# Linear attention beside a gated product: one ones column per four heads in kv, q projected one tile sooner, tile 0's epsilon on VectorE

## The chip, the cores and the metric

The kernel runs on one core of a Trainium2 chip. The time is device microseconds for one execution of the whole program. Before the change three runs gave 221.94, 222.10 and 222.32 us, with a median of 222.1 us.

## What is computed

The input x has 2048 tokens of 512 numbers in bf16. It is normalised per token, and the result feeds two branches whose outputs are added to x.

```
xn = (x - mean) / sqrt(var + 1e-5)
# branch A: linear attention, 32 heads of 16
q, k, v = split(xn @ wqkv)
phi(t)  = concat(softmax(t @ w_phi), softmax(-t @ w_phi))   # 32 features per head
kv  = sum over tokens of phi(k)^T v        # per head 32 x 16
z   = sum over tokens of phi(k)            # per head 32
o   = (phi(q) @ kv) / (phi(q) @ z + 1e-6)
A   = o @ wo
# branch B: gated product, hidden width 1792
B   = ((xn @ w_gate) * (xn @ w_up)) @ w_down
out = x + A + B
```

## The kernel before

The 2048 tokens are 16 tiles of 128 tokens (`NT = 16`). All instructions are issued in an order written out by hand: within each engine they run in the order in which the Python code names them, and an engine whose next instruction waits does nothing else meanwhile. The output of matrix products goes to PSUM: a pool `ps_s` gives six banks in rotation to every projection (`bank(...)`), and two more banks belong first to the kv accumulators (`ps_k`) and later to the numerators (`ps_ab`).

**Start.** Tiles 0 to 3 are normalised one by one: VectorE takes sums (L155, `stats`) and the mean and variance (L347, `mv`); GpSimd adds epsilon (L164, `ve`) and raises to the power -0.5 (L166, `rstd`); VectorE applies both (L171, `xn`). TensorE transposes the tile (L213, `tp`), and ScalarE copies it out (L215, `xnT`). Ten matmuls on zeros (`warm`, L307) keep TensorE running while x arrives.

**Stage k and v.** For each tile `vproj` projects v and evicts it into a buffer `vt` (L322; five buffers, with ones columns set once, L138). `kproj` computes the features of k. `kv(n)` then adds phi(k)^T v over the tokens into PSUM: eight matmuls (L333), one per group of four heads. Group `gr` has the 4 x 32 = 128 features of its heads as rows. Its 68 columns are, for each of the four heads, 16 columns of v and a column of ones, which gives z. Between these steps stand "units" of branch B (`ffn(k)`): a unit is eight matmuls (`g` and `u`, L275), a copy of g on ScalarE (L279, `g_sb`) and a product on VectorE (L280, `hT`).

**Turn to the numerators.** After the last kv, two VectorE products (L419) multiply the accumulators by a mask M4 that keeps each row's own head, and write `KV` to SBUF with 17 columns per head. Then come `qproj(4)`, one unit, and the numerators' stage. There `attend(n)` computes eight matmuls of 68 columns (L430) into `ab`, of which there is one buffer (two banks). VectorE then adds 1e-6 to the denominators (L435, `den`), takes reciprocals (L437, `rden`) and writes the quotient (L439, `otok`). A DMA transposes that into `oT` (L442).

**q.** `qproj(n)` takes the features of q: four matmuls (L240), two exponentials on ScalarE (L248 and L249, `e`), sums and reciprocals on VectorE (L252 `sums`, L254 `rs`), the product on GpSimd (L256, `phiq`), and a transposing DMA on SyncE's queue (L263) into one of six `phiqT` buffers. q of tiles 0 to 3 is made among the last k and v tiles.

**Numerators' stage.** The loop at its end is:

```
for n in range(NT):
    attend(n)
    if n + 5 < NT:
        qproj(n + 5)
    if n < 2:
        ffn(2 - n)
        continue
    fin(n - 2)
    if n >= 4:
        ffn(2)
```

`fin(n)` adds the products of `hT` with w_down and of `oT` with wo (L293, L296, 18 matmuls of 512 columns), adds x on VectorE (L299, `o_sb`) and stores the tile (L300).

Of the kernel before, what the change touches and what calls it, by code (L numbers as in the profile page):

```python
# [8 lines left out]
BF16 = mybir.dt.bfloat16  # L9
F32 = mybir.dt.float32  # L10
AF = mybir.ActivationFunctionType
ALU = mybir.AluOpType
# [4 lines left out]
def _bcast_ap(ap_in: bass.AP, new_ap):  # L17
    return bass.AP(tensor=ap_in.tensor, offset=ap_in.offset, ap=new_ap)
# [3 lines left out]
def kernel(  # L22
# [12 lines left out]
    nc = tc.nc  # L35
    P = 128
# [3 lines left out]
    DH = D // H  # L40
    NT = S // P
    DC = D // P
    FC = F // P
    EPS = 1e-5
    GT = 4
    NGRP = NT // GT
    TT = GT * P
    E1 = DH + 1

    def token_views(ap):  # L50
        rows = ap.flatten_outer_dims()
        first = rows[0:TT, :].rearrange("(n p) d -> p n d", p=P)
        rest = rows[TT:S, :].rearrange("(p n) d -> p n d", p=P)
        return lambda lo, hi: first[:, lo:hi, :] if hi <= GT else rest[:, lo - GT:hi - GT, :]
# [4 lines left out]
    consts = ctx.enter_context(tc.tile_pool(name="consts", bufs=1))  # L59
# [27 lines left out]
    for lo in (0, 2):  # L87
        nc.sync.dma_start(out=wv[:, lo:lo + 2, :],
                          in_=A_wqkv[lo * P:(lo + 2) * P, 2 * D:3 * D].rearrange("(c p) f -> p c f", p=P))
# [27 lines left out]

    BO = consts.tile([P, 8, E1], BF16)
    nc.gpsimd.memset(BO[:], 1.0)
    _block_rows(nc.gpsimd, BO[:], 8, DH, E1)  # L120
    NG = H // 4
    KV = wpool.tile([P, NG, 4, E1], BF16)
    M4 = consts.tile([P, 4, E1], BF16)

# [9 lines left out]
    NV = 5  # L134
    vts = []
    for i in range(NV):
        vt = consts.tile([P, 8, 4, E1], BF16, name=f"vt{i}")
        nc.vector.memset(vt[:, :, :, DH:E1], 1.0)  # L138
        vts.append(vt)

    gpool = ctx.enter_context(tc.tile_pool(name="gpool", bufs=3))
# [17 lines left out]
        stats = ln_sums(n)  # L159
        nc.vector.bn_aggr(out=mv, in_=stats[:])  # L160

    def ln_rstd(mv, k):
        ve = lnpool.tile([P, GT], F32, name="ve")
        nc.gpsimd.tensor_scalar(out=ve[:, 0:k], in0=mv[:, 0:k, 1], scalar1=EPS, scalar2=None, op0=ALU.add)  # L164
        rstd = lnpool.tile([P, GT], F32, name="rstd", bufs=GT)
        nc.gpsimd.tensor_tensor(out=rstd[:, 0:k], in0=ve[:, 0:k], in1=mhalf[:, 0:k], op=ALU.pow)  # L166
        return rstd
# [92 lines left out]
    def qproj(n):  # L260
        phiq = features(n, W1q, "q")
        phiqTs[n] = qtpool.tile([P, NG, P], BF16, name="phiqT")
        nc.sync.dma_start(out=phiqTs[n][:], in_=phiq[:].rearrange("p g c -> p (g c)"), transpose=True)  # L263
# [18 lines left out]
    def ffn(k):  # L282
        for _ in range(k):
            if units:
                unit(*units.pop(0))
# [23 lines left out]
    warm_up(10)  # L309

    with tc.tile_pool(name="ps_k", bufs=1, space=PSUM) as ps_k:
        kvps = [ps_k.tile([P, 4, 4, E1], F32, name=f"kv{b}") for b in range(2)]
        phiks = {}

        def vproj(n, copy=nc.scalar.copy, amid=None, later=False):
            ps = bank("pv")
            proj(ps, n, wv, range(2))
            if amid is not None:
                amid()
            proj(ps, n, wv, range(2, DC))  # L320
            def evict():
                copy(out=vts[n % NV][:, :, :, 0:DH], in_=ps.rearrange("p (a b c) -> p a b c", a=8, b=4))  # L322
            if later:
                return evict
            evict()

        def kproj(n):
            phiks[n] = features(n, W1k, "k")

        def kv(n):  # L330
            vt, phik = vts[n % NV], phiks[n]
            for gr in range(NG):
                nc.tensor.matmul(kvps[gr // 4][:, gr % 4, :, :].rearrange("p a b -> p (a b)"),  # L333
                                 lhsT=phik[:, gr, :], rhs=vt[:, gr, :, :].rearrange("p a b -> p (a b)"),
                                 start=(n == 0 and gr % 4 == 0), stop=(n == NT - 1 and gr % 4 == 3))

        mvs = [mv_tile() for n in range(GT)]
        rstds = []

        def first_apply(n):  # L340
            ln_apply(n, mvs[n][:, 0, 0:1], rstds[n][:, 0:1])

        def first_stats(n, amid=None):
            stats = ln_sums(n)
            if amid is not None:
                first_apply(amid)
            nc.vector.bn_aggr(out=mvs[n][:, 0, :], in_=stats[:])  # L347
            rstds.append(ln_rstd(mvs[n], 1))

        first_stats(0)  # L350
        first_stats(1)
        first_apply(0)
        first_stats(2, amid=1)
        first_stats(3, amid=2)
        first_apply(3)
        make_bd()
        nc.gpsimd.tensor_tensor(out=M4[:], in0=BO[:, 0:4, :], in1=BO[:, 4:8, :], op=ALU.add)
        lt(0, parts=2)
        warm_up(1)
        vproj(0, amid=lambda: lt(1, parts=2))  # L360
        copy_v = vproj(1, later=True)
        lt(2)
        copy_v()
        unit(0, 0, 0, 2 * P)
        vproj(2, copy=nc.vector.tensor_copy, amid=lambda: lt(3))
        unit(0, 1, 0, 2 * P)
        vproj(3, copy=nc.vector.tensor_copy)
        for f in range(2):
            unit(0, f, 2 * P, TT)
        del units[0:2]  # L370
        ffn(1)
        for j0 in (0, 2):
            fold(1, W1k, j0, (nc.scalar.copy, nc.vector.tensor_copy))
        ffn(1)
        ln_block(4)
        ffn(1)
        chore(2)
        kproj(0)
        ffn(1)
        chore(2)  # L380
        ffn(1)
        chore()
        kproj(1)
        ffn(1)
        chore()
        ffn(1)
        kproj(2)
        chore()
        ffn(1)
        kv(0)  # L390
        chore()
        ffn(1)
        kproj(3)
        chore()
        ffn(1)
        kv(1)
        nc.sync.dma_start(out=wT2[:, 0, :, :], in_=A_wqkv[:, 0:D], transpose=True)
        for n in range(GT, NT):
            if n in (4, 8):
                ln_block(n + 4)  # L400
            vproj(n)
            kproj(n)
            chore(1 if n % GT < 2 else 0)
            ffn(1)
            kv(n - 2)
            chore((1, 2, 2, 2)[n % GT])
            if n >= 8 and n % 2 == 0:
                qproj((n - 8) // 2)
            if n == 6:
                fold(0, W1q, 0)  # L410
            ffn(1)
            if n == 6:
                fold(0, W1q, 2)
        ffn(1)
        kv(NT - 2)
        ffn(1)
        kv(NT - 1)
        for b in range(2):
            nc.vector.tensor_tensor(out=KV[:, 4 * b:4 * b + 4, :, :], in0=kvps[b][:],  # L419
                                    in1=_bcast_ap(M4[:], [M4[:].ap[0], [0, 4], [E1, 4], [1, E1]]), op=ALU.mult)  # L420
        qproj(4)
        ffn(1)

    with tc.tile_pool(name="ps_ab", bufs=1, space=PSUM) as ps_ab, \
            tc.tile_pool(name="dp", bufs=2) as dpool:

        def attend(n):
            ab = ps_ab.tile([P, 2, TT], F32, name="ab")
            for gr in range(NG):
                nc.tensor.matmul(ab[:, gr // 4, (gr % 4) * 4 * E1:(gr % 4 + 1) * 4 * E1],  # L430
                                 lhsT=phiqTs[n][:, gr, :], rhs=KV[:, gr, :, :].rearrange("p a b -> p (a b)"),
                                 start=True, stop=True)
            abv = ab[:, :, 0:16 * E1].rearrange("p b (h j) -> p b h j", j=E1)
            den = dpool.tile([P, 2, 16], F32, name="den")
            nc.vector.tensor_scalar(out=den[:], in0=abv[:, :, :, DH], scalar1=1e-6, scalar2=None, op0=ALU.add)  # L435
            rden = dpool.tile([P, 2, 16, 1], F32, name="rden")
            nc.vector.reciprocal(out=rden[:, :, :, 0], in_=den[:])  # L437
            o_tok = dpool.tile([P, D], BF16, name="otok")
            nc.vector.tensor_tensor(out=o_tok[:].rearrange("p (b h d) -> p b h d", b=2, d=DH),  # L439
                                    in0=abv[:, :, :, 0:DH], in1=rden[:].to_broadcast((P, 2, 16, DH)), op=ALU.mult)  # L440
            oTs[n] = otpool.tile([P, DC, P], BF16, name="oT")
            nc.sync.dma_start(out=oTs[n][:], in_=o_tok[:], transpose=True)  # L442

        for n in range(NT):
            attend(n)
            if n + 5 < NT:
                qproj(n + 5)
            if n < 2:
                ffn(2 - n)
                continue  # L450
# [3 lines that stand above are left out]
        ffn(len(units))  # L454
        fin(NT - 2)
        fin(NT - 1, cuts=(0, 3 * P, D))
# [30 lines left out]
```

## Time and profile before

| | value |
|---|---|
| median of three runs | 222.1 us |
| the profiled execution's own time | 221.94 us |
| its span, first to last instruction | 220.2 us |
| TensorE busy | 214.5 us (97%) |
| VectorE busy | 138.4 us (63%) |
| ScalarE busy | 88.2 us (40%) |
| GpSimd busy | 72.1 us (33%) |
| mean granted TensorE clock | 0.998 |

The stages lie in the span as follows; the columns are busy us of each engine in that stretch, from the trace by windows.

| stretch, us | what runs | TensorE | VectorE | ScalarE | GpSimd |
|---|---|---|---|---|---|
| 0 to 8.3 | start | 6.62 | 4.84 | 3.31 | 4.36 |
| 8.3 to 109.2 | v, k, kv, units, q 0 to 3 | 100.27 | 70.44 | 61.68 | 44.51 |
| 109.2 to 111.7 | KV, q 4, one unit | 2.45 | 1.41 | 1.14 | 0.00 |
| 111.7 to 119.6 | attend 0 and 1, q 5 and 6, three units | 7.85 | 7.56 | 4.14 | 3.87 |
| 119.6 to 138.5 | attend from 2 on, fin | 18.80 | 12.78 | 4.43 | 7.74 |
| 138.5 to 188.9 | attend, q, fin, two units per tile | 50.14 | 30.00 | 13.54 | 11.61 |
| 188.9 to 217.5 | attend, fin | 28.41 | 11.10 | 0.00 | 0.00 |

A timeline line gives the start in us, the duration in us, the engine (PE is TensorE, PEld its weight loads, DVE is VectorE, ACT is ScalarE, POOL is GpSimd, SP is SyncE), the line of the code and the tiles. What stands in brackets is the engine's idle time before it and what ended it. A matmul's duration includes its way through the array; the start of the next one tells how long it holds the engine.

### The profile page before, as it was taken

What the parts mean: (1) busy time and instruction counts of PE and PEld (TensorE: products, weight loads), DVE (VectorE), ACT (ScalarE), POOL (GpSimd) and SP (SyncE); (2) the same over time, 40 slices, a digit from 0 to 9 for tenths busy, and PEclk for the clock granted to TensorE, in tenths of its full rate; (3) what the DMA queues carried; (4) which work ended last, traced back from release to release, by engine and by line L of the source; (5) the groups of instructions that cost most, each with busy time, mean ns of one, the idle gap of its engine ahead of it and who ended that gap; (6) DMA issues with size and microseconds to landing.
All of it is one profiled execution on the core that took longest, in us unless ns stands there. A gap on an engine that the chain in (4) does not pass through costs nothing.

```text
span 220.2 us, 3489 instructions
## 1 busy us (share of the span) xinstructions
PE 214.5 (97%) x1285; PEld 104.4 (47%) x1309; DVE 138.4 (63%) x237; ACT 88.2 (40%) x162; POOL 72.1 (33%) x62
## 2 busy tenths in 40 slices
PE   7999999999999999999999999999999999999995
PEld 2564444445444444444544444444444444454443
DVE  5657985885579685756589964197655745445321
ACT  2635486559755876545354221231322323100000
POOL 5300555455336653536333633033033033000000
PEclk9999999999999999999999999999999999999999
DMA  5999994404201223010205945214431431522611
GB/s 171 261 306 383 368 225 59 95 1 49 49 0 33 42 54 65 18 34 0 48 1 100 119 95 113 58 24 95 98 72 24 95 71 27 91 53 71 69 30 48
DMA packets 47233, 19.91 MB, mean 90 GB/s; under 512 B 37488, under 2 KB 46960, under 8 KB 47088
## 3 DMA queue, kind: packets, MB, share of 16 engines
q1 hardware_dynamic: 47216, 19.69, 39.6%
q8 instruction: 10, 0.16, 0.3%
q14 instruction: 7, 0.06, 0.1%
HBM read 8.67 MB, written 2.10 MB: 49 GB/s over the span
## 4 chain that ended last, share of the span: by engine, by line
PE 94%; DVE 2%; DMA 1%; issue 1%; POOL 0%; ACT 0%; DVEq 0%
PE fin L293 22%; PE u L275 22%; PE g L275 21%; PE fin L296 6%; PE pv L240 6%; PE q L240 6%; PE k L240 6%; PE ab L430 2%; PE kv L333 2%; DMA xall<-in_A_x_dram 1%; DVE stats L155 1%; PE pq L231 1%; DVE sums L252 1%; PE tp L213 0%; DVE hT L280 0%
## 5 line engine op out<-in xcount | busy, mean ns | idle before, releaser
L275 PE MATMUL u<-xnT,wu 128*128 128x512 bf16 (+1 forms) x229 | 57.7, 372 | 0.4
L275 PE MATMUL g<-xnT,wg 128*128 128x512 bf16 (+1 forms) x222 | 56.7, 371 | 0.4
L280 DVE TENSOR_TENSOR hT<-u,g_sb 128x512 bf16<-128x512 f32 (+1 forms) x58 | 37.4, 649 | 27.3 <-PE u L275 18.0
L279 ACT CAST g_sb<-g 128x512 bf16<-128x512 f32 (+1 forms) x58 | 33.3, 573 | 48.2 <-PE g L275 48.1
L252 DVE TENSOR_REDUCE sums<-e 128x64 f32<-128x1024 f32 x32 | 38.9, 1215 | 20.7 <-ACT e L249 20.7
L293 PE MATMUL fin<-wd,hT 128*128 128x512 bf16 (+2 forms) x234 | 50.9, 366 | 0.3
L256 POOL TENSOR_TENSOR phiq<-e,rs 128x1024 bf16<-128x1024 f32 x16 | 31.0, 1935 | 61.4 <-DVE rs L254 53.1
L256 POOL TENSOR_TENSOR phik<-e,rs 128x1024 bf16<-128x1024 f32 x16 | 30.9, 1934 | 48.2 <-DVE rs L254 46.2
L275 PEld LDWEIGHTS <-wu 128*128 128x128 bf16 x232 | 22.6, 98 | 25.7
L293 PEld LDWEIGHTS <-hT 128*128 128x128 bf16 x238 | 22.4, 98 | 24.8
L275 PEld LDWEIGHTS <-wg 128*128 128x128 bf16 x232 | 21.9, 98 | 23.4
L240 PEld LDWEIGHTS <-xnT 128*128 128x128 bf16 x192 | 17.3, 97 | 18.2 <-ACT xnT L215 1.1
L299 DVE TENSOR_TENSOR o_sb<-fin,xall 128x512 bf16<-128x512 f32 (+2 forms) x17 | 11.2, 656 | 22.3 <-PE fin L296 22.2
L248 ACT ACTIVATE e<-q 128x512 f32<-128x512 f32 x16 | 9.5, 596 | 26.1 <-PE q L240 20.7
L254 DVE RECIPROCAL rs<-sums 128x64 f32<-128x64 f32 x32 | 17.7, 553 | 3.1
L240 PE MATMUL pv<-wv,xnT 128*128 128x512 bf16 x62 | 16.4, 379 | 0.4 <-ACT xnT L215 0.2
L296 PE MATMUL fin<-wo,oT 128*128 128x512 bf16 (+2 forms) x68 | 16.6, 366 | 0.0
L240 PE MATMUL k<-W1k,xnT 128*128 128x512 bf16 x63 | 16.2, 379 | 0.0
L240 PE MATMUL q<-W1q,xnT 128*128 128x512 bf16 x60 | 15.9, 378 | 0.1
L322 ACT CAST vt<-pv 128x512 bf16<-128x512 f32 x14 | 8.3, 591 | 10.9 <-PE pv L240 10.9
L248 ACT ACTIVATE e<-k 128x512 f32<-128x512 f32 x16 | 9.6, 597 | 7.0 <-PE k L240 6.6
L439 DVE TENSOR_TENSOR otok<-ab,rden 128x512 bf16<-128x512 f32 x16 | 11.1, 691 | 0.6
(46 smaller groups left out, 117.4 us busy)
## 6 DMA issues: line engine op xcount, KB each, us to landing
out_dram<-o_sb SPq DMA_DIRECT2D x15, 128.0 KB, 1.9
wd<-in_B_w_down_dram SPq DMA_DIRECT2D x1, 1792.0 KB, 15.4
wg<-in_B_w_gate_dram SPq DMA_DIRECT2D x2, 640.0 KB, 7.0
wu<-in_B_w_up_dram SPq DMA_DIRECT2D x2, 640.0 KB, 8.1
xall<-in_A_x_dram SPq DMA_DIRECT2D x1, 1024.0 KB, 12.0
wv<-in_A_wqkv_dram SPq DMA_DIRECT2D x2, 256.0 KB, 3.9
wg<-in_B_w_gate_dram SPq DMA_DIRECT2D x2, 256.0 KB, 4.9
wu<-in_B_w_up_dram SPq DMA_DIRECT2D x2, 256.0 KB, 5.3
```

The costliest lines, as they stand in the source:

```text
L240: nc.tensor.matmul(ps, lhsT=xnT[:, j, n * P:(n + 1) * P], rhs=w[:, j, :], start=(j == 0), stop=(j == DC - 1))
L248: nc.scalar.activation(out=e[:, :, 0, :], in_=pfv, func=AF.Exp, scale=1.0)
L252: nc.vector.tensor_reduce(out=sums[:], in_=ev, axis=AX.X, op=ALU.add)
L254: nc.vector.reciprocal(out=rs[:].rearrange("p a b -> p (a b)"), in_=sums[:])
L256: nc.gpsimd.tensor_tensor(out=phi[:].rearrange("p g (x f) -> p (g x) f", f=DH), in0=ev, in1=rs[:].to_broadcast((P, 2 * H, DH)), op=ALU.mult)
L275: nc.tensor.matmul(ps, lhsT=w[:, c, f * P:(f + 1) * P], rhs=xnT[:, c, T * TT + lo:T * TT + hi], start=(c == 0), stop=(c == DC - 1))
L279: nc.scalar.copy(out=g_sb[:, 0:hi - lo], in_=pss[0])
L280: nc.vector.tensor_tensor(out=hTs[T][:, f, lo:hi], in0=pss[1], in1=g_sb[:, 0:hi - lo], op=ALU.mult)
L293: nc.tensor.matmul(ps, lhsT=hTs[T][:, f, t4 * P:(t4 + 1) * P], rhs=wd[:, f, lo:lo + w], start=(f == 0), stop=False)
L296: nc.tensor.matmul(ps, lhsT=oTs[n][:, c, :], rhs=wo[:, c, lo:lo + w], start=False, stop=(c == DC - 1))
L299: nc.vector.tensor_tensor(out=o_sb[:], in0=ps, in1=xall[:, n, lo:lo + w], op=ALU.add)
L439: nc.vector.tensor_tensor(out=o_tok[:].rearrange("p (b h d) -> p b h d", b=2, d=DH), in0=abv[:, :, :, 0:DH], in1=rden[:].to_broadcast((P, ...
```

## The change

Three edits. `vt` gets 65 columns per group of four heads, 64 of v and one of ones, so that a kv matmul has 65 columns in place of 68. The mask step then makes the 16 columns per head and the z column in two VectorE instructions for each accumulator, four in place of two. `qproj(5)` is called ahead of `attend(0)`, and after each `attend(n)` stands `qproj(n + 6)` in place of `qproj(n + 5)`. The epsilon of tile 0 is added by VectorE; that of all other tiles stays on GpSimd.

```diff
+    G1 = 4 * DH + 1
...
-        vt = consts.tile([P, 8, 4, E1], BF16, name=f"vt{i}")
-        nc.vector.memset(vt[:, :, :, DH:E1], 1.0)
+        vt = consts.tile([P, NG, G1], BF16, name=f"vt{i}")
+        nc.vector.memset(vt[:, :, 4 * DH:G1], 1.0)
...
-    def ln_rstd(mv, k):
+    def ln_rstd(mv, k, eng=nc.gpsimd):
         ve = lnpool.tile([P, GT], F32, name="ve")
-        nc.gpsimd.tensor_scalar(out=ve[:, 0:k], in0=mv[:, 0:k, 1], scalar1=EPS, scalar2=None, op0=ALU.add)
+        eng.tensor_scalar(out=ve[:, 0:k], in0=mv[:, 0:k, 1], scalar1=EPS, scalar2=None, op0=ALU.add)
...
-                copy(out=vts[n % NV][:, :, :, 0:DH], in_=ps.rearrange("p (a b c) -> p a b c", a=8, b=4))
+                copy(out=vts[n % NV][:, :, 0:4 * DH], in_=ps.rearrange("p (g x) -> p g x", g=NG))
...
-                nc.tensor.matmul(kvps[gr // 4][:, gr % 4, :, :].rearrange("p a b -> p (a b)"),
-                                 lhsT=phik[:, gr, :], rhs=vt[:, gr, :, :].rearrange("p a b -> p (a b)"),
+                nc.tensor.matmul(kvps[gr // 4][:, gr % 4, :], lhsT=phik[:, gr, :], rhs=vt[:, gr, :],
...
-        first_stats(0)
+        first_stats(0, eng=nc.vector)
...
-            nc.vector.tensor_tensor(out=KV[:, 4 * b:4 * b + 4, :, :], in0=kvps[b][:],
-                                    in1=_bcast_ap(M4[:], [M4[:].ap[0], [0, 4], [E1, 4], [1, E1]]), op=ALU.mult)
+            kvb, m4, z = KV[:, 4 * b:4 * b + 4, :, :], M4[:], kvps[b][:, :, 4 * DH:G1]
+            nc.vector.tensor_tensor(out=kvb[:, :, :, 0:DH],
+                                    in0=kvps[b][:, :, 0:4 * DH].rearrange("p g (h d) -> p g h d", h=4),
+                                    in1=_bcast_ap(m4, [m4.ap[0], [0, 4], [E1, 4], [1, DH]]), op=ALU.mult)
+            nc.vector.tensor_tensor(out=kvb[:, :, :, DH], in0=_bcast_ap(z, [z.ap[0], [G1, 4], [0, 4]]),
+                                    in1=_bcast_ap(m4, [m4.ap[0], [0, 4], [E1, 4]]), op=ALU.mult)
         qproj(4)
         ffn(1)
+        qproj(5)
...
             attend(n)
-            if n + 5 < NT:
-                qproj(n + 5)
+            if n + 6 < NT:
+                qproj(n + 6)
```

More of the change, by code (lines that the diff above doesn't have):

```diff
@@ L311 @@
     with tc.tile_pool(name="ps_k", bufs=1, space=PSUM) as ps_k:
-        kvps = [ps_k.tile([P, 4, 4, E1], F32, name=f"kv{b}") for b in range(2)]
+        kvps = [ps_k.tile([P, 4, G1], F32, name=f"kv{b}") for b in range(2)]
         phiks = {}
@@ L341, in first_apply, with first_stats @@
             ln_apply(n, mvs[n][:, 0, 0:1], rstds[n][:, 0:1])
-        def first_stats(n, amid=None):
+        def first_stats(n, amid=None, eng=nc.gpsimd):
             stats = ln_sums(n)
@@ L347, in first_stats @@
             nc.vector.bn_aggr(out=mvs[n][:, 0, :], in_=stats[:])
-            rstds.append(ln_rstd(mvs[n], 1))
-        first_stats(0)
+            rstds.append(ln_rstd(mvs[n], 1, eng))
+        first_stats(0, eng=nc.vector)
         first_stats(1)
```

## The prediction

> **What bounds the kernel now.** I read the page's busy times and its chain first.
>
> ```profile
> PE 214.5 (97%) x1285; PEld 104.4 (47%) x1309; DVE 138.4 (63%) x237; ACT 88.2 (40%) x162; POOL 72.1 (33%) x62
> ...
> PE 94%; DVE 2%; DMA 1%; issue 1%; POOL 0%; ACT 0%; DVEq 0%
> ```
>
> TensorE carries the chain. From 8.3 us to the end its matmuls follow one another at 0.216 us for 512 columns. So the time moves in three ways only: fewer columns, an earlier start, or a new hole in this stream, which nothing later repays. Next, the timeline of the start:
>
> ```profile
> 3.63 0.18 DVE L347 BATCH_NORM_AGGREGATE mv<-stats 128x2 f32<-128x6 f32 x1
> 3.90 0.24 POOL L164 TENSOR_SCALAR ve<-mv 128x1 f32<-128x1 f32 x1 [1.50 <-DVE mv L347]
> 4.22 0.58 POOL L166 TENSOR_TENSOR rstd<-ve,mhalf 128x1 f32<-128x1 f32 x1
> 4.84 0.41 DVE L171 TENSOR_SCALAR xn<-xall,mv,rstd 128x512 bf16<-128x512 bf16 x1 [0.23 <-POOL rstd L166]
> 5.31 0.40 PE L213 MATMUL tp<-ident,xn 128*128 128x128 bf16 x4 [0.19 <-DVE xn L171]
> ```
>
> Tile 0's normalisation is a strict sequence that ends TensorE's first wait. Last, the timeline of the turn from kv to the numerators, where q moves:
>
> ```profile
> 110.06 0.78 DVE L419 TENSOR_TENSOR KV<-kv,M 128x272 bf16<-128x272 f32 x2
> ...
> 110.56 0.60 ACT L248 ACTIVATE e<-q 128x512 f32<-128x512 f32 x1 [1.45 <-PE q L240]
> 111.05 0.59 ACT L249 ACTIVATE e<-q 128x512 f32<-128x512 f32 x1
> ...
> 111.68 1.22 DVE L252 TENSOR_REDUCE sums<-e 128x64 f32<-128x1024 f32 x1 [0.84 <-ACT e L249]
> ...
> 112.03 0.42 PE L430 MATMUL ab<-KV,phiqT 128*128 128x68 bf16 x8
> ...
> 113.00 0.55 DVE L254 RECIPROCAL rs<-sums 128x64 f32<-128x64 f32 x1
> ...
> 113.47 0.63 DVE L280 TENSOR_TENSOR hT<-u,g_sb 128x512 bf16<-128x512 f32 x1
> ...
> 114.02 0.18 DVE L435 TENSOR_SCALAR den<-ab 128x32 f32<-128x32 f32 x1
> 114.23 0.35 DVE L437 RECIPROCAL rden<-den 128x32 f32<-128x32 f32 x1
> 114.61 0.69 DVE L439 TENSOR_TENSOR otok<-ab,rden 128x512 bf16<-128x512 f32 x1
> ...
> 115.22 1.21 DVE L252 TENSOR_REDUCE sums<-e 128x64 f32<-128x1024 f32 x1
> ...
> 117.00 1.22 DVE L280 TENSOR_TENSOR hT<-u,g_sb 128x512 bf16<-128x512 f32 x2
> ...
> 118.14 0.18 DVE L435 TENSOR_SCALAR den<-ab 128x32 f32<-128x32 f32 x1
> ...
> 118.75 0.69 DVE L439 TENSOR_TENSOR otok<-ab,rden 128x512 bf16<-128x512 f32 x1
> ...
> 119.55 0.32 PEld L430 LDWEIGHTS <-phiqT 128*128 128x128 bf16 x8 [0.45 <-issue]
> 119.58 0.42 PE L430 MATMUL ab<-KV,phiqT 128*128 128x68 bf16 x8
> ```
>
> VectorE runs without a break from 111.68 on: 7.56 us busy of the 7.90 us from 111.7 to 119.6. And attend(2) starts 0.14 us after otok(1) has ended (118.75 + 0.69 = 119.44), while its preceding matmul was done streaming at 119.44 as well. There is one `ab` buffer, so attend(n + 1) may start only when otok(n) has read it. Here VectorE and TensorE arrive together. This is the hidden second bound, and the change puts a q's VectorE work in front of it.
>
> **q one tile sooner.** I count in the clock of the profile before. TensorE does q(5) at 112.03, four matmuls in 0.86 us, so attend(0) is at 112.89. With 0.26 for its eight matmuls, q(6) is at 113.15, and two units (four times 0.86) run from 114.01 to 117.46, when attend(1) is due.
>
> VectorE's order becomes: sums(4), rs(4), hT, sums(5), rs(5), den(0), rden(0), otok(0), sums(6), rs(6), hT, hT, den(1), rden(1), otok(1). Up to hT nothing moves. sums follows the first matmul of its q by 111.68 - 109.44 = 2.24 us, so sums(5) starts at 112.03 + 2.24 = 114.27, though VectorE is free from 114.02. The steps from one start to the next are taken from the rows above: sums to rs 1.31, rs to the next 0.47, den to otok 0.59 to 0.61, otok to sums 0.61, two hT to den 1.14.
>
> - den(0) at 114.27 + 1.31 + 0.47 = 116.05; otok(0) at 116.64, ending 117.33; attend(1) can start 0.14 later, at 117.47. It was due at 117.46: no loss, no slack.
> - sums(6) at 117.25, rs(6) 118.56, hT 119.03, den(1) 120.17, otok(1) 120.78, ending 121.47; attend(2) can start at 121.61.
> - TensorE after attend(1): 117.47 + 0.26 + 0.86 (q 7) + 1.73 (a unit) = 120.32. It waits 1.29 us.
>
> Before, the same attend(2) stood at 119.58, and the 0.86 us of q moved ahead of it would put it at 120.44. The loss is 121.61 - 120.44 = **+1.17 us**. Behind the waiting matmuls stand q(8), fin(0) and everything else of TensorE, so it is lost for good.
>
> What is late next: attend(3). TensorE needs 0.26 + 0.86 + 18 x 0.216 = 5.01 us after attend(2), to 126.62; VectorE's den(2) and otok(2) follow sums(7), rs(7) and one hT and end at 125.02, so 1.6 us are spare. Later VectorE is busy 12.78 of 18.90 us and less. The q that the end of the loop no longer does leaves tile 10 shorter by the same 0.86 us of TensorE: moved, not saved. The last q's exponentials, GpSimd product (1.94 us) and DMA move with it, off the path.
>
> Queues: on SyncE's queue phiqT(5) now stands ahead of oT(0). GpSimd's product for q(5) ends at about 116.13 + 0.14 + 1.94 = 118.2, so oT(0) is issued at about 119.5 in place of 116.97; a transpose took 1.2 to 2.1 us there, and fin(0) needs it at 121.87 + 0.86 + 3.02 = 125.75. Hidden by 4 us. phiqT(n + 6) takes the buffer that attend(n) has just read, long before its own product is ready. PSUM's six banks: the tightest reuse is q(8) at 121.87 on the bank that the first of the two hT at 119.03 frees at 119.7. Free.
>
> **The KV step.** Two products of 272 elements, 0.35 to 0.43 us each, become two of 256 (0.33 to 0.43) and two of 16, for which the nearest rows are a `vt` memset (0.085 us) and den from PSUM (0.21 to the next). Together 0.83 to 1.28 us from 110.06, so at most to 111.34; VectorE was idle until 111.68. I take nothing. If they cost over 1.87 us the excess would go into the wait: sums(4) at 111.68 can slip by 0.25 before sums(5) does.
>
> [...]
>
> **65 columns.** The eight kv matmuls of a tile hold TensorE 109.44 - 109.18 = 0.26 us, 32 ns each; a 128-column matmul holds it 55 ns (tp). So a column is worth (55 - 32)/60 = 0.38 ns, and 128 matmuls by 3 columns give **-0.15 us**. If 32 ns is a floor it is nothing; with the 512-column rate of 0.42 it is 0.16. Bounds -0.20 and 0.
>
> **Epsilon on VectorE.** ve leaves GpSimd, where it costs 4.22 - 3.90 = 0.32 us up to rstd. On VectorE it waits for mv (3.81), starts near 3.85 and takes 0.06 (a small memset) to 0.18 us (mv); with the 0.09 us from VectorE to GpSimd, rstd starts at 4.00 to 4.12. But stats(1), mv(1) are now about 0.22 us later on VectorE, so xn(0) follows mv(1) at about 4.74, not 4.84: **-0.10 us**, bounds -0.20 and +0.10 (were the dependent ve as slow as on GpSimd). xn(1) goes to 5.86, ending 6.27, and tile 1's weight load would be at 6.30: just hidden. The memsets and the copies into `vt` (0.588 us on ScalarE, 0.694 on VectorE) keep or lose elements and have idle time around them: nothing.
>
> **Sum.** 1.17 - 0.15 - 0.10 = +0.92 us on the profiled execution's 221.94 (span 220.2 and 1.75 around it): 222.86. That run lies 0.16 under the median, so 223.0 to compare with 222.1.
>
> **The rivals.**
>
> *The cover works.* The extra 0.86 us of TensorE work ahead of each attend hides VectorE, all waits at attend vanish, and with -0.14 (attend(2)'s present wait), -0.15 and -0.10 the time is 221.7 on the median's scale. For it: TensorE does gain 0.86 us before attend(0). Against: VectorE gets 1.78 us of sums and rs in front of den(0), and the 0.25 us of idle time. It decides at 120.18: otok(1) must end by then, so that VectorE does 7.20 us of rows in 5.91.
>
> *A smaller hole.* If sums(5) overlaps more and the wait is cut to 0.6, the sum is +0.2 to +0.4: 222.4, within noise.
>
> *The clock goes too.* The granted clock is 1.00 in every stretch of the profile, and no idle time of TensorE there exceeds 0.3 us once it runs. At the start the ten warm matmuls took 3.88 us, 0.39 each in place of 0.216. Should the new hole bring that state back for such a stretch, about 1.6 us more: 224.6. [...]
>
> *The change not taking effect.* The lists of each engine's instructions show 65 columns, the moved q and ve on VectorE; I give this nothing.
>
> **Numbers.** The forecast has 0.80, the cover 0.10 (split into 0.04 faster by over 0.2%, 0.06 within), the smaller hole 0.05, clock or a dear KV step 0.05. A difference of 0.2%, 0.44 us, is about what a measurement of this kernel can tell from none. So faster 0.04, same 0.11, slower 0.85. The range: the hole less 0.25 (sums(5) without its wait), with -0.20 and -0.20, gives 222.6; the smaller hole brings it down to 222.3. Above, +0.10 at the start, no gain on columns and 0.3 of KV excess give 223.7.
>
> **What would show it.** In the profile after: TensorE idle 1.1 to 1.4 us before attend(2), with VectorE otok(1) ending just ahead; attend(1) with almost no wait; kv matmuls at 31 ns; rstd(0) near 4.1 us. I am wrong if attend(2) does not wait, if VectorE is idle between sums(5) and otok(1), or if a later attend waits too.

## The result, and the profile after

The changed kernel takes 223.33 us (median of six runs, 223.04 to 223.71), where six runs of the kernel before give 222.21: 1.0053 times as long, 95% interval 1.0038 to 1.0067, which is 0.8 to 1.5 us. The medians lie 1.12 us apart; the sum of the prediction had asked for 0.92 us, and its range of 222.3 to 223.7 us holds the result.

The profiled execution took 223.41 us with a span of 221.7. The chain's line in its page has changed where the hole is:

```profile
PE 92%; DVE 5%; issue 1%; ACT 1%; DVEq 0%; ACTq 0%
```

VectorE, 2% of the chain before, now holds 5%, because the chain leaves TensorE at attend(2). This is the timeline there:

```profile
112.03 1.22 DVE L253 TENSOR_REDUCE sums<-e 128x64 f32<-128x1024 f32 x1 [0.27 <-ACT e L250]
...
113.24 0.42 PE L435 MATMUL ab<-KV,phiqT 128*128 128x68 bf16 x8
...
114.62 1.22 DVE L253 TENSOR_REDUCE sums<-e 128x64 f32<-128x1024 f32 x1 [0.17 <-ACT e L250]
...
116.41 0.13 DVE L440 TENSOR_SCALAR den<-ab 128x32 f32<-128x32 f32 x1
...
116.96 0.69 DVE L444 TENSOR_TENSOR otok<-ab,rden 128x512 bf16<-128x512 f32 x1
...
117.57 1.21 DVE L253 TENSOR_REDUCE sums<-e 128x64 f32<-128x1024 f32 x1
...
117.81 0.42 PE L435 MATMUL ab<-KV,phiqT 128*128 128x68 bf16 x8
...
119.35 1.22 DVE L281 TENSOR_TENSOR hT<-u,g_sb 128x512 bf16<-128x512 f32 x2
...
120.49 0.18 DVE L440 TENSOR_SCALAR den<-ab 128x32 f32<-128x32 f32 x1
...
121.09 0.69 DVE L444 TENSOR_TENSOR otok<-ab,rden 128x512 bf16<-128x512 f32 x1
...
121.89 0.32 PEld L435 LDWEIGHTS <-phiqT 128*128 128x128 bf16 x8 [1.57 <-issue]
121.93 0.41 PE L435 MATMUL ab<-KV,phiqT 128*128 128x68 bf16 x8 [1.11 <-DVE otok L444]
```

VectorE has no gap from the second sums to otok(1). otok(1) ends at 121.09 + 0.69 = 121.78, and attend(2) starts 0.15 us later. Its preceding matmul began at 120.44 and held TensorE 0.216 us, so by the starts the wait is 121.93 - 120.66 = 1.27 us (the bracket says 1.11, since it counts idle time from the modelled end of a matmul). Before it was 0.14. attend(1) and attend(3) do not wait. That is +1.13 us.

The rest of this execution's longer span comes ahead of the hole, where kv and all that follows it stand 0.35 us later than in the profile before. 0.31 us of that arise at the start:

```profile
4.74 0.38 DVE L172 TENSOR_SCALAR xn<-xall,mv,rstd 128x512 bf16<-128x512 bf16 x1
...
5.18 0.40 PE L214 MATMUL tp<-ident,xn 128*128 128x128 bf16 x4
...
6.48 0.39 PE L214 MATMUL tp<-ident,xn 128*128 128x128 bf16 x4
...
7.30 1.45 PE L241 MATMUL pv<-wv,xnT 128*128 128x512 bf16 x6 [0.43 <-ACT xnT L216]
```

xn(0) comes at 4.74 and tp(0) at 5.18, both 0.10 to 0.13 us sooner, and tile 1's transposes too (6.48 for 6.61). But the third matmul of pv(0), which reads wv's second half, starts at 7.30 in place of 6.99. The bracket names xnT, but tile 0's copies into xnT had ended at 6.26 us (5.61 + 0.65). What came last is the DMA of wv's second half: by the trace it was issued at 2.69 us in both executions and landed at 7.26 here and at 6.95 before, and the matmul follows 0.04 us later in both. Whether the change made it land late was open, and the experiments had to tell.

### The profile page after: what moved, and what is told of

It is laid out like the page before. It is cut to its first block, busy times and chain, and to the rows that moved or that the text cites. A ratio compares the mean times of both kernels' runs of the same rounds, so it can differ in the third digit from the quotient of the medians.

```text
span 221.7 us, 3486 instructions
## 1 busy us (share of the span) xinstructions
PE 214.6 (97%) x1285; PEld 104.7 (47%) x1309; DVE 138.5 (62%) x240; ACT 88.3 (40%) x162; POOL 72.0 (32%) x61
## 4 chain that ended last, share of the span: by engine, by line
PE 92%; DVE 5%; issue 1%; ACT 1%; DVEq 0%; ACTq 0%
PE fin L294 22%; PE u L276 21%; PE g L276 20%; PE fin L297 6%; PE pv L241 6%; PE k L241 6%; PE q L241 5%; PE kv L334 2%; PE warm L308 2%; PE ab L435 2%; DVE sums L253 2%; DVE hT L281 1%; DVE otok L444 1%; PE pq L232 1%; DVE rs L255 1%
## 5 line engine op out<-in xcount | busy, mean ns | idle before, releaser
L156 DVE BATCH_NORM_STATS2 stats<-xall 128x6 f32<-128x512 bf16 x16 | 10.7, 667 | 1.5 <-DMA xall<-in_A_x_dram 1.5
```

Source lines behind the costliest of these rows:

```text
L156: nc.vector.bn_stats(out=stats[:], in_=xall[:, n, :])
```

## Experiments

**One part at a time.** Each of three kernels is the kernel before with one of the edits and nothing else; their diffs are parts of the one above.

*q one tile sooner.*

> The kernel before with q one tile sooner and nothing else. Hole theory: the whole loss is TensorE's wait for otok(1) at attend(2), 1.27 us in the profile after against 0.14 before, so this kernel loses all of it: +1.1 us, about 223.3 for 222.2, with that wait in its trace. Rival, the loss is partly at the start (pv(0)'s second half began 0.31 us later in the profile after) and comes from the epsilon edit: then this kernel loses only 0.8 us, about 223.0.

223.58 us against 222.29: ratio 1.0062, interval 1.0049 to 1.0074. The timeline at attend(2):

```profile
120.92 0.69 DVE L440 TENSOR_TENSOR otok<-ab,rden 128x512 bf16<-128x512 f32 x1
...
121.73 0.32 PEld L431 LDWEIGHTS <-phiqT 128*128 128x128 bf16 x8 [1.58 <-issue]
121.76 0.41 PE L431 MATMUL ab<-KV,phiqT 128*128 128x68 bf16 x8 [1.11 <-DVE otok L440]
```

The same wait, 1.28 us by the starts, with the start of the kernel before. q alone makes the whole loss, 1.1 to 1.6 us by the interval; the rival, 0.8 us with a share for the epsilon edit, falls.

*65 columns, and the four KV products.*

> The kernel before with the 65 columns and the four KV products and nothing else. As predicted: -0.15 us, 222.05, eight kv matmuls held 0.25 us or less. Rival, 32 ns per kv matmul is a floor, as the profile after suggests (0.26 us for eight at 65 columns too): 0.0 us, 222.2. A rival of loss: the four KV products, 1.0 us in the profile after in place of 0.78, delay sums(4) and so attend(2): no more than +0.1.

222.37 us against 222.29: ratio 1.0004, interval 0.9995 to 1.0013, no gain. By the starts, eight kv matmuls hold TensorE 259 ns (median over the 16 tiles), where those of 68 columns take 257. The four KV products start 110.69 to 111.44 and cost 0.97 us in place of 0.78; VectorE is still idle for 0.66 us before sums(4).

*Tile 0's epsilon on VectorE.*

> The kernel before with tile 0's epsilon on VectorE and nothing else. As predicted: -0.10 us. wv theory: the second half of wv lands at about 7.0 us or later and sets pv(0)'s second half whatever tile 0 does, so xn(0) and the first pv matmul come 0.10 to 0.13 us sooner and pv(0)'s third matmul does not: 0.0 us, 222.2. Rival, the edit itself makes that matmul late (7.30 for 6.99): +0.3 us, 222.5.

222.04 us against 222.29: ratio 0.9996, interval 0.9987 to 1.0006, nothing that can be told from zero. Its start shows why it need not pass on:

```profile
1.24 4.45 PE L307 MATMUL warm<-zeros 128*128 128x512 bf16 x10 [1.24 <-DVE zeros L104]
...
4.71 0.38 DVE L171 TENSOR_SCALAR xn<-xall,mv,rstd 128x512 bf16<-128x512 bf16 x1
...
5.48 0.63 PE L213 MATMUL tp<-ident,xn 128*128 128x128 bf16 x4
```

xn(0) is ready at 5.09, and tp(0) starts at 5.48: in this execution the ten warm matmuls took 4.45 us, not 3.88, and tp(0) is queued behind them.

**TensorE's part of q sooner, VectorE's part where it was.**

> The kernel before with TensorE's and ScalarE's part of q (matmuls and exponentials) one tile sooner, but VectorE's sums and reciprocals, GpSimd's product and the DMA of that q where they were. VectorE's order around attend is then that of the kernel before. Hole theory: VectorE's work put in front of den makes the hole, so no wait at attend(2) is left, and the 0.14 us of the kernel before goes too: 222.05 for 222.2. Rival, the hole comes of TensorE's or ScalarE's part coming sooner (banks, the e buffers): +0.5 us or more, with a wait before attend(2) still.

```diff
     def qproj(n):
+        qhead(n); qtail(n)          # qhead: matmuls and exponentials; qtail: the rest
...
         ffn(1)
+        qhead(5)
...
             attend(n)
             if n + 5 < NT:
-                qproj(n + 5)
+                qtail(n + 5)
+            if n + 6 < NT:
+                qhead(n + 6)
```

222.19 us for 222.29, ratio 0.9995 (0.9986 to 1.0004), and no wait before any attend:

```profile
119.48 0.69 DVE L455 TENSOR_TENSOR otok<-ab,rden 128x512 bf16<-128x512 f32 x1
...
120.63 0.50 PEld L446 LDWEIGHTS <-phiqT 128*128 128x128 bf16 x8
120.85 0.42 PE L446 MATMUL ab<-KV,phiqT 128*128 128x68 bf16 x8
```

otok(1) ends at 120.17, 0.68 us ahead of attend(2). TensorE and ScalarE do here what they do in the kernel with q alone; only VectorE's, GpSimd's and the DMA's order differs. So the hole does not come from the matmuls or exponentials. Of the three that moved it is VectorE whose work stands in front of den without a gap, and the next experiment takes away the buffer through which it acts. Even so the old 0.14 us are all that can be won, and that is below what the runs resolve.

**Two ab buffers.** The next kernels have plain DMAs where the transposing ones stood; a base shows what that does.

> A base for three others: the kernel before with every transposing DMA replaced by a plain DMA of as many bytes, so transposition by DMA is left out of what is computed; all else stands. Nothing of it lies in the first 7 us, so the start should look as before: pv(0)'s third matmul at 7.0 to 7.6 us. The time is near that before, 222 to 223, since the DMAs are off the path.

222.37 us against 222.35, ratio 0.9998 (0.9990 to 1.0007), and the 0.14 us before attend(2) as before: the DMAs are off the path, and the base can stand for the kernel before.

> The kernel after with plain DMAs in place of the transposing ones (transposition by DMA left out), with two ab buffers (four banks) and four banks for the projections in place of six. Hole theory: attend(2) waits for the one ab buffer, so its wait of 1.27 us goes, whatever four banks cost elsewhere. Rival, attend(2) waits for KV, phiqT or a queue: 1.2 us or more stay there. Four banks may move a wait to the units or q next to it: then the hole is VectorE's lateness and shows wherever its first unread bank is.

```diff
-    ps_s = ctx.enter_context(tc.tile_pool(name="ps_s", bufs=6, space=PSUM))
+    ps_s = ctx.enter_context(tc.tile_pool(name="ps_s", bufs=4, space=PSUM))
...
-    with tc.tile_pool(name="ps_ab", bufs=1, space=PSUM) as ps_ab, \
+    with tc.tile_pool(name="ps_ab", bufs=2, space=PSUM) as ps_ab, \
```

```profile
120.93 1.03 PE L276 MATMUL g<-xnT,wg 128*128 128x512 bf16 x4
...
121.35 1.22 DVE L281 TENSOR_TENSOR hT<-u,g_sb 128x512 bf16<-128x512 f32 x2
...
122.03 1.02 PE L276 MATMUL u<-xnT,wu 128*128 128x512 bf16 x4
...
122.89 0.42 PE L435 MATMUL ab<-KV,phiqT 128*128 128x68 bf16 x8
...
123.09 0.69 DVE L444 TENSOR_TENSOR otok<-ab,rden 128x512 bf16<-128x512 f32 x1
```

attend(2) now starts before otok(1) does, and has no wait: what it waited for was the one ab buffer. VectorE is as late as ever, and a part of it shows at the next bank instead: the unit's u starts 1.10 us after its g, 0.24 more than four matmuls take, while hT still reads banks. The single run took 224.37 us, for with four banks TensorE also waits 0.65 us at 16.6, 0.34 at 30.3 and 0.81 at 53.1. Six banks and one ab is the better split here.

**What a kv matmul costs.**

> The 65-column kernel of the second experiment with plain DMAs as in the base, and kv matmuls of 33 columns: the first 32 columns of v in each group of four heads are left out and their accumulators hold zeros. Read from the trace alone. Floor theory: a weight load and a small matmul hold TensorE 32 ns however few the columns, so eight kv matmuls still take 0.25 to 0.26 us. Rival, columns count at 0.4 ns each and 3 of them merely did not show: eight take about 0.15 us.

> The 65-column kernel of the second experiment, with plain DMAs as in the base, but with the groups 68 elements apart in vt and in the accumulators, so that each group starts where it did before and only 65 of 68 columns are streamed. Eight kv matmuls took 257 ns at 68 columns, 259 at 65 in steps of 65, 205 at 33. Theory that steps of 65 elements cost what 3 columns gain: eight take about 245 ns, -0.15 to -0.2 us in all. Floor theory, pairs of this size are held by something else than columns: 255 to 260 ns, 0.0 us.

```diff
-        vt = consts.tile([P, NG, G1], BF16, name=f"vt{i}")
+        vt = consts.tile([P, NG, 4 * E1], BF16, name=f"vt{i}")
...
-        kvps = [ps_k.tile([P, 4, G1], F32, name=f"kv{b}") for b in range(2)]
+        kvps = [ps_k.tile([P, 4, 4 * E1], F32, name=f"kv{b}") for b in range(2)]
...
-                nc.tensor.matmul(kvps[gr // 4][:, gr % 4, :], lhsT=phik[:, gr, :], rhs=vt[:, gr, :],
+                nc.tensor.matmul(kvps[gr // 4][:, gr % 4, 0:G1], lhsT=phik[:, gr, :], rhs=vt[:, gr, 0:G1],
```

The last kv of each kernel and the matmul after it, in the timelines of TensorE: 65 columns in steps of 65,

```profile
109.81 0.42 PE L334 MATMUL kv<-vt,phik 128*128 128x65 bf16 x8
110.07 1.02 PE L241 MATMUL q<-W1q,xnT 128*128 128x512 bf16 x3
```

65 in steps of 68,

```profile
109.74 0.41 PE L334 MATMUL kv<-vt,phik 128*128 128x65 bf16 x8
109.99 1.02 PE L241 MATMUL q<-W1q,xnT 128*128 128x512 bf16 x4
```

and 33 columns:

```profile
108.50 0.36 PE L336 MATMUL kv<-vt,phik 128*128 128x33 bf16 x8
108.71 1.02 PE L241 MATMUL q<-W1q,xnT 128*128 128x512 bf16 x4
```

Eight take 259, 250 and 205 ns (257 with 68 columns before), as medians over the 16 tiles of one profile each. Such medians repeat within 1 ns: all nine profiles with 68 columns have 256 or 257, all three with 65 in steps of 65 have 259 or 260. So 32 ns is no floor; whether 25 ns, the step between most of the 33-column ones, is one was not tried. In steps of 68 the three columns bring 7 ns per eight, 16 x 7 = 0.11 us, near the 0.15 predicted; in steps of 65 that gain is lost. The starts within a group of eight show where: in steps of 68 they alternate between 29 and 33 ns, in steps of 65 they are all at 32 to 33 from the third on. In the changed kernel, too, the 2 ns per eight that steps of 65 cost against 68 columns are 0.03 us of the 0.35 by which it reached the hole later. Whether the step in `vt` (bf16) or the one in the accumulators (f32) makes the difference was not tried. In the time of the whole kernel 0.11 us stays unseen: ratio 0.9995 (0.9984 to 1.0005). The single run with 33 columns took 221.21 us.

**What bounds the start.**

> The base with plain DMAs, and with the DMA of x for tiles 2 and 3 issued after both halves of wv, so that wv's second half is issued 0.47 us sooner. wv theory: its landing sets pv(0)'s third matmul (6.99 to 7.63 us in the profiles so far, with xn(0) moving by 0.1 only), so that comes to 6.9 or sooner and the time falls by some 0.3 us against the base, unless tile 2, now later, takes its place. Rival, tile 1's xnT or ScalarE sets it: 0.0.

```diff
-    dma_x(2, 4)
     for lo in (0, 2):
         nc.sync.dma_start(out=wv[:, lo:lo + 2, :], ...
+    dma_x(2, 4)
```

> The same with tile 0's epsilon on VectorE too, transposition by DMA left out as in the base. wv theory: with wv in time, tile 0's normalisation bounds the start again, so the 0.1 us that xn(0) gains passes on: -0.1 us against the same kernel without the epsilon edit. Rival, wv still sets pv(0)'s third matmul, or tile 1's chain, which the edit makes 0.1 us later, does: 0.0.

Both missed: 223.33 and 223.29 us against 222.35, ratios 1.0048 (1.0034 to 1.0062) and 1.0059 (1.0036 to 1.0081), slower by about 1 us. wv's second half did land sooner, at 5.68 us in the first, but x for tile 2 landed at 6.55 in place of 4.60. The timeline of the first:

```profile
6.57 0.69 DVE L155 BATCH_NORM_STATS2 stats<-xall 128x6 f32<-128x512 bf16 x1 [1.21 <-DMA xall<-in_A_x_dram]
...
7.18 0.40 DVE L171 TENSOR_SCALAR xn<-xall,mv,rstd 128x512 bf16<-128x512 bf16 x1
```

stats(2) waits for the x that now comes later, and xn(1), which needs no more data, is queued behind it on VectorE: 7.18 in place of 5.77. It is the same pattern as at attend: a ready instruction behind one that waits. In the two profiled executions this costs 0.33 us at pv(0)'s third matmul (7.87 for the base's 7.54), and they are 0.34 us apart; how the 1 us of the medians divides was not taken apart. So this order of DMAs cannot show what wv costs. Taking wv's second half away from tile 0 can:

> The base with plain DMAs, and tile 0's v made with wv's first half twice, so pv(0) does not need wv's second half (tile 0's v is wrong by that). wv theory: pv(0)'s third matmul follows tile 1's transposes at once, 6.85 us with xn(0) at 4.84, where the profiles with the start of before had 6.99 to 7.63; the time falls by 0.3 us or so against the base. Rival, something else holds it: 0.0 and the same 7.0 to 7.6.

```diff
-            proj(ps, n, wv, range(2, DC))
+            for j in range(2, DC):
+                nc.tensor.matmul(ps, lhsT=xnT[:, j, n * P:(n + 1) * P], rhs=wv[:, j - 2 if n == 0 else j, :], ...
```

> The same with tile 0's epsilon on VectorE. wv theory: with that wait gone tile 0's normalisation sets the start, and its 0.10 us pass on: third matmul near 6.75, -0.1 us against the same kernel without the epsilon edit. Rival, tile 1's chain, 0.13 us later by the edit (xn(1) at 5.9), takes over: 0.0.

222.27 and 222.29 us against 222.35, ratios 0.9994 (0.9985 to 1.0004) and 0.9995 (0.9986 to 1.0004): no measurable gain from either. In the trace of the second the third matmul of pv(0) follows tile 1's transposes at once, and the next DMA is late in its place:

```profile
6.56 0.39 PE L213 MATMUL tp<-ident,xn 128*128 128x128 bf16 x4
...
6.79 0.59 PE L321 MATMUL pv<-wv,xnT 128*128 128x512 bf16 x2
...
9.36 0.61 PE L275 MATMUL u<-xnT,wu 128*128 128x256 bf16 x4 [0.24 <-DMA wu<-in_B_w_up_dram]
```

In this execution wv's second half landed at 7.34 us, 0.55 after the start of the matmul that no longer reads it; wu landed at 9.31 (8.92 in the profile before), and u waits 0.41 us by the starts. In the first kernel's execution the warm matmuls took 4.45 us again and tp(0) stood at 5.48.

The landings by the trace settle what held pv(0)'s third matmul. In four profiles wv was in time, and the matmul starts 0.22 to 0.23 us after the first of tile 1's transposes: q alone (wv landed at 6.55 us), epsilon alone (6.92), the base (7.04) and two ab buffers (6.75). In six wv came later, and the matmul follows its landing by 0.04 to 0.05 us: before (6.95), changed (7.26), 65 columns (7.59), split q (7.54), 33 columns (7.12) and steps of 68 (7.67). The split q has the epsilon of the kernel before, and its profile names the DMA:

```profile
7.59 1.46 PE L240 MATMUL pv<-wv,xnT 128*128 128x512 bf16 x6 [0.60 <-DMA wv<-in_A_wqkv_dram]
```

So wv's landing varies from execution to execution by more than 1 us without the epsilon edit, and 7.26 in the changed kernel lies within that.

## Why the prediction was right, and where it was wrong

**The hole: right, and to 0.04 us.** Shifted by the 0.35 us of this execution's start, the steps were sums(5) 114.62, den(0) 116.40, otok(0) 116.99, den(1) 120.52, otok(1) 121.13 and attend(2) 121.96. Measured: 114.62, 116.41, 116.96, 120.49, 121.09 and 121.93. The wait was put at 1.29 us and is 1.27; net +1.13 for +1.17. That is shown by q alone (all of the loss), by VectorE's order restored (no wait), and by two buffers (no wait at attend). attend(1) without a wait and attend(3) with time to spare came as written.

**The rivals: fell.** TensorE's extra 0.86 us covers VectorE only if VectorE's own part of q stays behind den, as the split shows. The smaller hole did not come either: sums(5) waited for its exponentials as worked out, 0.17 us by the bracket.

**65 columns, -0.15 us: a term that failed.** The bound "nothing" was right and the value taken was not: 259 ns for eight is 32.4 ns per matmul, where 31 had been named as a sign. The value was interpolated between rows of 68 and 128 columns, and the edit also changed the step between groups; with the step kept at 68 it is -0.11 by the starts.

**Epsilon, -0.10 us: the term that did not pass on.** xn(0) moved by 0.10 us, as worked out, and rstd(0) started at 4.09. But the prediction took tile 0's normalisation to be all that stands before TensorE's stream. In the profile before tp(0) does follow xn(0), yet pv(0)'s third matmul already waits 0.16 us for wv (landed at 6.95, start at 6.99), so a gain of 0.10 ends there. And in eight of the fourteen profiles of this study the warm matmuls were slow to the end and tp(0) stood at 5.48, whatever xn(0) did. With both terms at zero the sum is +1.13 to +1.17, which the interval of 0.8 to 1.5 holds; 0.92 lay in that interval too, since the two terms are small beside the hole.

**The KV step: hidden, as said.** 0.97 us for the 0.83 to 1.28 worked out. VectorE's idle time before sums(4) shrank from 0.84 to 0.27 us in the changed kernel, more than the products explain: the hT before them started 0.38 us later relative to its unit, and its bracket names the kv matmuls behind the unit in place of the unit's u. In the kernel with 65 columns alone that hT waits for u as before. Why was not tried; more than some 0.5 us of further delay (0.27, and 0.25 ahead of sums(5)) would have lengthened the hole.

**The clock: did not fall.** The matmuls after the hole stand 0.216 us apart. The granted clock, which the prediction read, would not tell the two rates apart: the view by windows prints 1.00 also for 1.2 to 4.2 us of the profile before, where the warm matmuls stand 0.427 us apart, and the first record of the clock in that trace begins only at 4.41 us.

## What to carry to other kernels

A step moved ahead brings all its engines' work along: count it in every in-order queue that it passes (xn(1) behind the waiting stats(2): 7.18 us for 5.77), and where a buffer has a single copy, look for the instruction that frees it and for what now stands in front of that one (here `ab` and otok(1), +1.13 us). If only one engine's part is wanted sooner, split the step and move that part. A gain read from one profile's critical chain is safe only if the next bound, here a DMA and the warm-up behind it, is further off than the gain.

## What the runs showed of the hardware

TensorE reached its full rate, 0.216 us for 512 columns, at different times in different executions. The ten warm matmuls took from 3.8 to 4.45 us; at the slow rate they stand 0.427 us from one to the next, and in the slowest executions the first two matmuls of pv(0) were still 0.40 us apart at 6.6 to 7.0 us. Full rate came 3.0 us after the first warm matmul with q alone (the one at 4.20 us held TensorE 0.22 us), and nearly 6 us after it in the base (the one at 6.98 still held it 0.33 us). What sets that time was not shown. With the landing of the first DMAs (wv's second half at 6.55 to 7.67 us in the ten profiles above) this spread may be the source of the 0.6 to 1.0 us by which equal runs of this kernel differ; that was not taken apart.

A step of 65 elements between groups in place of 68 cost 9 ns per eight matmuls of 65 columns (259 for 250), more than the 7 ns that three columns fewer gain (250 for 257).
